# Delta-rule attention into a mixture of attention experts: the fourth unit's Gram products made during the first substitution, wide fillers and a new instruction order

## Chip, cores and metric

The kernel runs on 1 core of one Trainium2 chip. The metric is the device time in microseconds (us) of one execution. The engines are PE (matmul), DVE, ACT, POOL and SP; SP issues nearly all transfers.

## What is computed

```
k_n = k / (norm(k) + 1e-6)                          # q, k, v: [4, 8, 768, 48]
for t in range(768):
    y[t]  = q[t] @ state                            # state: 48 x 48 for each batch and head
    state = state + beta[t] * outer(k_n[t], v[t] - k_n[t] @ state)
x = y laid out as [4, 768, 384]
for e in range(4):                                  # experts with 64 features
    a   = softmax(causal(scale * (x wq[e]) (x wk[e])^T))
    out += gate[e] * (a @ (x wv[e]) @ wo[e])        # gate: softmax over the top 2 of 4 of x w_gate
```

## The kernel before

The 32 pairs of batch and head times 768 tokens are cut into **six units** n = 0 to 5. A unit is 256 tokens of half of the batch: units 0, 1, 2 are one half in order of time, units 3, 4, 5 the other half. A unit has four chunks c of 64 tokens, and its 32 tiles (8 pairs of heads times 4 chunks) lie side by side.

For each unit the kernel loads the keys (`le`) into one of three row tiles `GF[n % 3]`, so that units 0 and 3 share `GF[0]`; PE makes the Gram products of the keys of each chunk (`ga` for units 0 to 2, `gb` for 3 to 5: two calls k = 0, 1 of two chunks each); ACT brings them back into the row tile (`ge`); diagonal blocks of 32 x 32 go to a tile `DA` (`gd`, four transfers) and by a DVE transpose to `B` (`bi`); norms and the factor `aa` come from the diagonal (`nm`).

Then each 32 x 32 block is inverted by a **substitution** of 30 dependent steps. Unit 0's (`s0`) runs on DVE at the start, while nothing else can go on. Units 1 to 5 have theirs on POOL (`sv.n.0` scales, on POOL for unit 1 and on DVE for the others; `sv.n.1` to `sv.n.30` are two POOL tensor operations each, L508 and L510; `sv.1.31` masks on POOL; `sv.n.32`, in unit 2 on DVE, ends it), one unit ahead of the place where the result is wanted. Two DVE transposes (`bo` into `DG`, `tn` into `TN`) hand it to PE, and `m1`, `we`, `m2`, `me`, `tc` build the unit's inverse in the row tile.

The **scan** of a unit goes through its chunks in order, each depending on the state that the last one left: `gk` (PE: keys times queries and state), `xs` (DVE: x = v - ...), `tx` (PE), `us` (DVE, ACT), `ku` (PE), `se` (ACT: new state), `yy` (PE: outputs), `yh` and `yl` (ACT, DVE: high and low parts of the outputs into `XU[n % 2]` and `H3`), `hx` (transfers). `vs` on POOL scales v (tile `kv`) by the norms first; `lv` and `lt` load the two halves of `kv`, `lk` the keys, `lq` the queries.

The **experts** of a unit follow a unit later, woven into the next scans: `pj` (projections; `kh`, `kl` evict them as high and low parts), `pv` (values and gate; `ve`, `lg` evict), `mx` to `mo` (row maxima), `sc`, `ex`, `av` (scores, exponentials, products with v), `ft`, `fo`, `so` (output). Their weights come in by `ww` (load), `wh` (high part, ACT) and `wl` (low part, POOL L312), for seven pieces.

**Fillers**: a word `fl.k` issues k matmuls of zeros (`ZB`, bf16, 128 x 128) on PE, into a bank that nobody reads. There are 883 of them: 487 ahead of the end of the first substitution (379 in one train that spans most of it), 396 later.

**What sets the order.** The whole program is a table of 1783 words, `ORDER`, written out one word for each call of a function above; digits behind an @ are the PSUM banks. A loop at the end of `tile_kernel` runs them one by one under `manual_schedule`, so each engine and the one queue of SP execute their instructions exactly in the order of the table:

```
for word in ORDER.split():
    word, _, at_ = word.partition("@")
    name, *a = word.split(".")
    ...
    steps[name](*a)
```

An instruction that has to wait holds up everything behind it on its engine or queue. The waits themselves follow from the tiles that are read and written.

Of the kernel before, what the change touches and what calls it, by code (L numbers as in the profile page):

```python
# [899 lines left out]
```

## Time and profile before

| | us |
|---|---|
| timed runs | 426.77, 424.69, 426.94; median 426.77 |
| profiled execution | 421.56, of it 419.8 span |
| PE busy | 399.7 (95%) |
| DVE, ACT, POOL busy | 302.8, 205.7, 227.0 |

The profiled execution is 1.2% below the median of the timed runs. PE's busy time holds the fillers, so a busy PE can stand for a wait. A stage of this kernel is best seen from one `m1.n.0` (the first product with the inverse of unit n's blocks) to the next: PE meets it at 46.9, 79.0, 138.4, 187.8, 254.4 and 306.4 us for units 0 to 5, and unit 1's first scan product `gk.1.0` at 89.6.

### The profile page before, as it was taken

To read this page: it belongs to the slowest core of one execution; us is meant where nothing else is said; L and a number is where in the kernel's file an instruction comes from. 1 tells how busy PE (TensorE), PEld (TensorE's weight loads), DVE (VectorE), ACT (ScalarE), POOL (GpSimd) and SP (SyncE) were. 2 spreads that over 40 slices of the span, in tenths; PEclk is the share of its full clock that TensorE was granted. 3 is DMA by queue.
4 is the path that set the end of the run, shared out by engine and by line. 5 is a ranking of instruction groups with operands and counts; after the bars stand their busy time and mean duration, and the time that the engine had idled before them with its cause. 6 is when DMAs were issued, how large, how long until landed. Compare 5 with 4: busy or idle time off the path is not lost.

```text
span 419.8 us, 20613 instructions
## 1 busy us (share of the span) xinstructions
PE 399.7 (95%) x9119; PEld 356.3 (85%) x9119; DVE 302.8 (72%) x635; ACT 205.7 (49%) x453; POOL 227.0 (54%) x415
## 2 busy tenths in 40 slices
...
GB/s 212 244 125 132 6 61 90 199 87 174 53 153 141 140 69 58 77 142 154 213 56 43 94 21 108 103 120 4 160 173 125 52 20 13 11 16 62 4 3 75
DMA packets 81657, 39.81 MB, mean 95 GB/s; under 512 B 64992, under 2 KB 74848, under 8 KB 81568
## 3 DMA queue, kind: packets, MB, share of 16 engines
...
q8 instruction: 71, 1.16, 1.1%
...
## 4 chain that ended last, share of the span: by engine, by line
PE 73%; DVE 10%; DMA 8%; SPq 3%; issue 3%; ACT 1%; POOL 1%; DVEq 0%; ACTq 0%
PE p L199 71%; DMA bt<-in_beta_dram 2%; DVE p L460 2%; DMA qp<-in_kq_dram 2%; DVE vs L459 1%; SPq L637 1%; DVE mp L730 1%; DMA at<-in_wqk_dram 1%; PE p L814 1%; DVE qp L395 1%; DMA kv<-in_kv_dram 1%; DMA at<-in_wo_dram 1%; PE p L739 1%; DVE p L725 1%; POOL wl L312 1%
## 5 line engine op out<-in xcount | busy, mean ns | idle before, releaser
L508 POOL TENSOR_TENSOR tm<-b 128x30 f32<-128x30 f32 (+9 forms) x150 | 72.9, 486 | 28.9 <-DVE b L504 18.1
L510 POOL TENSOR_TENSOR b<-b,tm 128x30 f32<-128x30 f32 (+9 forms) x150 | 77.7, 518 | 11.8
L199 PE MATMUL p<-zb 128*128 128x128 bf16 x883 | 55.9, 222 | 4.5 <-DVE zb L316 3.3
L775 ACT ACTIVATE at<-p 128x768 f32<-128x768 f32 (+1 forms) x48 | 43.3, 917 | 31.4 <-PE p L199 14.8
L199 PEld LDWEIGHTS <-zb 128*128 128x128 bf16 x883 | 50.7, 99 | 6.5 <-DVE zb L316 3.3
L201 ACT ACTIVATE qp<-p 64x192 f32<-64x192 f32 (+1 forms) x92 | 36.9, 401 | 26.0 <-PE p L199 24.6
L730 DVE TENSOR_REDUCE mp<-p 128x2 f32<-128x1024 f32 (+3 forms) x40 | 44.4, 1115 | 2.9 <-PE p L199 1.9
L199 PE MATMUL p<-vs,at 128*64 128x65 f32 x1344 | 44.9, 223 | 0.9 <-ACT at L775 0.9
L199 PEld LDWEIGHTS p<-vs,at 128*64 128x64 f32 x1344 | 41.4, 137 | 4.4 <-issue 2.0
L395 DVE TENSOR_TENSOR qp<-p,cs 64x256 f32<-64x256 f32 x96 | 40.5, 421 | 5.8 <-PE p L199 4.1
L199 PE MATMUL p<-xu,wh 128*128 128x512 f32 (+1 forms) x168 | 40.3, 373 | 0.0
L572 POOL TENSOR_TENSOR kv<-kv,nt 128x384 f32<-128x384 f32 x24 | 19.6, 831 | 31.2 <-DMA kv<-in_kv_dram 25.7
L199 PEld LDWEIGHTS p<-xu,wh 128*128 128x128 f32 x168 | 27.8, 188 | 5.8 <-issue 0.5
L199 PE MATMUL p<-qh,kh 64*128 64x128 f32 (+1 forms) x192 | 29.1, 299 | 0.2 <-DVE mp L730 0.2
L199 PE MATMUL p<-qp 128*48 128x64 f32 (+1 forms) x768 | 26.3, 221 | 2.2 <-issue 1.9
L780 DVE TENSOR_TENSOR p<-p,km 128x512 f32<-128x512 f32 x24 | 16.6, 696 | 14.6 <-PE p L199 14.2
L199 PE MATMUL p<-qh,kl 64*128 64x128 f32 (+1 forms) x192 | 26.9, 276 | 0.0
L199 PE MATMUL p<-ql,kh 64*128 64x128 f32 (+1 forms) x192 | 26.9, 276 | 0.0
L199 PE MATMUL p<-wh,xu 128*128 128x260 f32 x144 | 26.3, 294 | 0.6 <-DVE mp L730 0.6
L199 PEld LDWEIGHTS p<-qp 128*48 128x48 f32 (+1 forms) x768 | 23.0, 123 | 4.5 <-issue 2.8
L199 PE MATMUL p<-mr,sl 64*128 64x128 f32 (+1 forms) x192 | 26.7, 274 | 0.0
L199 PE MATMUL p<-qp,kf 48*64 48x112 f32 (+1 forms) x768 | 23.8, 259 | 0.3 <-issue 0.3
...
## 6 DMA issues: line engine op xcount, KB each, us to landing
...
```

Source lines behind the costliest of these rows:

```text
L199: T.matmul(o, lhsT=a, rhs=b, start=start, stop=True, skip_group_check=True)
L201: copy = lambda o, a: S.activation(o, a, AF.Copy)
L312: G.tensor_tensor(flat(WL[w])[:, i:i + n], st(k)[:, 0:n], flat(WH[w])[:, i:i + n], op=OP.subtract)
L395: V.tensor_tensor(QP[zi(n, c) % RQ][tok(f), f, 4 * x:4 * x + 4, 0:64], gv(n, c)[r, x, :, 0:64], PMK[r, None, :].to_broadcast([64, 4, 64]), ...
L459: V.tensor_tensor(tv, t, l, op=OP.mult)
L460: V.tensor_tensor(PX[:, 0:i, i + 1:], PX[:, 0:i, i + 1:], tv, op=OP.subtract)
L508: G.tensor_tensor(tv, b[:, i:i + 1, i + 1:].to_broadcast([128, i, m]), b[:, 0:i, i:i + 1].to_broadcast([128, i, m]), op=OP.mult)
L510: G.tensor_tensor(b[:, 0:i, i + 1:], b[:, 0:i, i + 1:], tv, op=OP.subtract if n == 1 else OP.add)
L572: G.tensor_tensor(vt, vt, NRM[n % 2][:, c * NP:c * NP + NP, None].to_broadcast([128, NP, HD]), op=OP.mult)
L730: V.tensor_reduce(o[:, :, y0:y0 + per], g, axis=AXL.X, op=OP.max, negate=True)
L775: S.activation(at(n, b, y, kp)[:, :, 0:w], P8[:, b0:b0 + 2, 0:w], AF.Exp, scale=0.125)
L780: V.tensor_tensor(g, g, KM[:, None, None, :].to_broadcast([128, 2, 2, 128]), op=OP.add)
```

## The change

1. **Unit 3's Gram products.** The loads, the products and their eviction (`le.3.*`, `gb.3.*`, `ge.3.*`) move from the scans of units 0 and 1 into the first substitution. `GF[0]` holds unit 0's inverse then, so they work in a tile `HO` that shares its memory with `XU[1]`, the second unit's output tile, which is free until unit 1's first `yh`. Four transfers `gm.3.c` (128 x 512, 2048 bytes a row, 256 KB each) copy `HO` to `GF[0]` in scan 0; `XU[1]` is allocated behind the last.
2. **Wide fillers.** `ZB` becomes 512 columns wide, and `fw.k` issues k matmuls of 128 x 512. There are 227 narrow and 144 wide fillers in place of the 883: PE's matmuls fall from 5791 to 5279, its explicit weight loads from 883 to 371. The long train becomes `fw.67` and `fl.7`.
3. **A new table** of 1809 words. `gk.0.0` (unit 0's first scan product) moves from the first substitution into scan 0, behind `ku.0.0`; `ex0` (which loads ACT's exponential table) goes there too, behind `gk.0.1`. Two memsets of PSUM banks 6 and 7 become one (`zp`). The rest are moves; three are shown below.

```
-sv.1.9 sv.1.10 bo.0 sv.1.11 tn.0 tc0.2.1 fl.379@7 m1.0.0@1 sv.1.12 ...
+sv.1.10 sv.1.11 tn.0 tc0.0.0 fw.67@7 fl.7@7 m1.0.1@1 m1.0.0@4 sv.1.12 ...
 ...
-    XU = [sb(f"xu{i}", 3, 2, 2, 2, 128, dt=F32R) for i in range(2)]
+    HO = cp.tile([128, 3072], F32, name="ho", tag="xu1")
+    XU = [sb("xu0", 3, 2, 2, 2, 128, dt=F32R), None]
 ...
-    ZB = sb("zb", 128, dt=BF16)
+    ZB = sb("zb", 512, dt=BF16)
 ...
+    def hold(n, k):
+
+        if n == 3:
+            return HO[:, 1024 * k:1024 * k + 1024].rearrange("p (m s) -> p m s", m=4)
+        return GF[n % RG][:, 16 * k:16 * k + 16].rearrange("p (m t) s -> p m (t s)", m=4)
+
 ...
-    V.memset(P8[:, 7], 0.0)
+    def zp():
+        V.memset(P8[:, 6:8], 0.0)
 ...
-            mm(P8[:, BK["fl", k][0], 0:128], ZB, ZB)
+            mm(P8[:, BK["fl", k][0], 0:128], ZB[:, 0:128], ZB[:, 0:128])
+
+    def fw(k):
+        for _ in range(k):
+            mm(P8[:, BK["fw", k][0], 0:512], ZB[:, 0:128], ZB)
 ...
     def le(n, c):
+        if n > 2:
+            nc.sync.dma_start(hold(n, c // 2)[0:112, 2 * (c % 2):2 * (c % 2) + 2],
+                              kq[n, c, 0:112, 0:512].rearrange("p (a b) -> p a b", a=2))
+            return
 ...
-                    mm(P8[gr(f, p), b + x, o:o + 64], a[feat(f), p], a[feat(f), p])
+                    a = hold(n, k)[feat(f), 2 * j + x, 64 * i:64 * i + 64]
+                    mm(P8[gr(f, p), b + x, o:o + 64], a, a)
 ...
+    def gm(n, c):
+        nc.sync.dma_start(GF[0][:, NP * c:NP * c + NP].rearrange("p t s -> p (t s)"), HO[:, 512 * c:512 * c + 512])
+        if c == 3:
+            XU[1] = cp.tile([128, 3, 2, 2, 2, 128], F32R, name="xu1", tag="xu1")
+
     def ge(n, k, x):
-        copy(half(GF[n % RG], k, x), gs(n, k, x))
+        if n > 2:
+            copy(hold(n, k).rearrange("p (c x) (i j) -> p c x i j", x=2, i=4)[:, :, x], gps(n, k, x))
+            return
+        copy(half(GF[n % RG], k, x), gps(n, k, x))
```

(`gs` is renamed `gps` throughout.) In the excerpts below, line numbers behind the change are 8 to 24 higher for the same function.

**POOL, start of unit 1's substitution.** L409 (L433 behind the change) is the last work for unit 0, L572 (L596) is `vs`, L312 (L320) is `wl`, L502 (L526) is `sv.1.0`, and L508 and L510 (L532, L534) are the steps. Before:

```order
L409 TENSOR_TENSOR at1_105<-at1_105,aa0_88 128x1024 x2
L572 TENSOR_TENSOR kv0_72<-kv0_72,nt0_93 128x384
L572 TENSOR_TENSOR kv1_73<-kv1_73,nt0_93 128x384
L312 TENSOR_TENSOR wl0_133<-at2_106,wh0_130 128x512
L502 TENSOR_TENSOR b1_81<-b1_81,aa1_92 128x1024
...
L510 TENSOR_TENSOR b1_81<-b1_81,tm_84 128x4x27
L312 TENSOR_TENSOR wl0_133<-at2_106,wh0_130 128x512 x2
L572 TENSOR_TENSOR kv2_74<-kv2_74,nt0_93 128x384
```

Behind the change:

```order
L320 TENSOR_TENSOR wl0_133<-at2_106,wh0_130 128x512
L433 TENSOR_TENSOR at1_105<-at1_105,aa0_88 128x1024 x2
L596 TENSOR_TENSOR kv0_72<-kv0_72,nt0_93 128x384
L596 TENSOR_TENSOR kv2_74<-kv2_74,nt0_93 128x384
L596 TENSOR_TENSOR kv1_73<-kv1_73,nt0_93 128x384
L526 TENSOR_TENSOR b1_81<-b1_81,aa1_92 128x1024
L532 TENSOR_TENSOR tm_84<-b1_81 128x30
```

`vs.0.2` (kv2) goes from the middle of the substitution to a place ahead of it, and one `wl` ahead of L433; the other two `wl` go between later steps.

**SP's queue, the loads of the first substitution.** `gf2` and `ho` are key tiles for Gram products, `kv` values, `at2` weight pieces. Before:

```order
L350 DMA gf2_77<-in_kq_dram 112x512
L281 DMA kv0_72<-in_kv_dram 128x384
L304 DMA at2_106<-in_wqk_dram 128x512
L281 DMA kv1_73<-in_kv_dram 128x384
L277 DMA qp3_71<-in_kq_dram 64x8x64 x2
L288 DMA cs_136<-in_consts_dram 128x209
L304 DMA at2_106<-in_wqk_dram 128x512 x2
L480 DMA da_79<-gf2_77 32x32x32 x4
L281 DMA kv2_74<-in_kv_dram 128x384
```

Behind the change:

```order
L366 DMA gf2_77<-in_kq_dram 112x512
L289 DMA kv0_72<-in_kv_dram 128x384 x2
L363 DMA ho_96<-in_kq_dram 112x512
L285 DMA qp0_68<-in_kq_dram 64x8x64 x2
L363 DMA ho_96<-in_kq_dram 112x512 x2
L285 DMA qp2_70<-in_kq_dram 64x8x64 x2
L296 DMA cs_136<-in_consts_dram 128x209
L285 DMA qp3_71<-in_kq_dram 64x8x64 x2
L289 DMA kv2_74<-in_kv_dram 128x384 x2
L312 DMA at2_106<-in_wqk_dram 128x512
```

Four `ho` loads (the first of them a few rows earlier) and the kv2 pair stand ahead of the weights; `kv2` used to come behind three weight pieces and `gd`.

**DVE, from the end of unit 1's substitution to unit 2's scaling.** L467 and L470 (L491, L494) are `bo.1` and `tn.1`, L575 (L599) `xs.0.3`, L661 (L685) `kl`, L395 (L419) `pm`, L629 and L631 (L653, L655) `yl`, L426 (L450) the first of unit 2's norms, behind which `sv.2.0` comes. Before:

```order
L467 STREAM_TRANSPOSE dg_78<-b1_81 128x32x32
L470 STREAM_TRANSPOSE tn_82<-b1_81 128x32x32
L575 TENSOR_TENSOR x_95<-kv0_72,p8_63 128x384
L661 TENSOR_TENSOR kl_100<-p8_63,kh_99 128x2x128
L395 TENSOR_TENSOR qp3_71<-p8_63,cs_136 64x4x64
L661 TENSOR_TENSOR ql_102<-p8_63,qh_101 128x2x128
L395 TENSOR_TENSOR qp3_71<-p8_63,cs_136 64x4x64 x3
L595 COPY qp3_71<-p8_63 64x4x48 x2
L426 TENSOR_SCALAR g00_85<-b0_80 128x32
```

Behind the change:

```order
L491 STREAM_TRANSPOSE dg_78<-b1_81 128x32x32
L494 STREAM_TRANSPOSE tn_82<-b1_81 128x32x32
L419 TENSOR_TENSOR qp3_71<-p8_63,cs_136 64x4x64
L685 TENSOR_TENSOR kl_100<-p8_63,kh_99 128x2x128
L599 TENSOR_TENSOR x_95<-kv0_72,p8_63 128x384
L419 TENSOR_TENSOR qp3_71<-p8_63,cs_136 64x4x64 x3
L653 TENSOR_TENSOR h3_98<-p8_63,h3_98 112x2x64
L655 TENSOR_TENSOR xu0_97<-p8_63,xu0_97 112x2x3x64
L685 TENSOR_TENSOR ql_102<-p8_63,qh_101 128x2x128
L450 TENSOR_SCALAR g00_85<-b0_80 128x32
```

Two `yl` of chunk 2 come ahead of unit 2's norms, which used to stand ahead of `sv.1.32`; a further L685 stands right ahead of `sv.2.0`.

## Rows read from the trace of the kernel before

**Rows 1.** From the page: the span; the busy time, share and instructions of each engine; the shares of the chain of work that ended last.

```profile
span 419.8 us, 20613 instructions
PE 399.7 (95%) x9119; PEld 356.3 (85%) x9119; DVE 302.8 (72%) x635; ACT 205.7 (49%) x453; POOL 227.0 (54%) x415
PE 73%; DVE 10%; DMA 8%; SPq 3%; issue 3%; ACT 1%; POOL 1%; DVEq 0%; ACTq 0%
```

**Rows 2.** Busy time by stage. Columns: stretch from:to and its length in us; busy us and number of instructions of PE, PE's weight loads, DVE, ACT, POOL; granted PE clock (1.00 is full); busy share of the DMA engines; GB/s.

```profile
3.20:26.50 23.30, 21.77 (x549) 20.77 (x550) 17.49 (x43) 12.61 (x30) 12.75 (x18) 1.00 0.88 224
25.20:46.40 21.20, 21.20 (x381) 21.10 (x379) 19.09 (x51) 4.62 (x9) 18.06 (x29) 1.00 0.40 92
46.90:79.00 32.10, 30.06 (x900) 27.46 (x900) 22.21 (x35) 17.62 (x47) 27.43 (x46) 1.00 0.29 83
79.00:89.60 10.60, 10.60 (x356) 9.77 (x356) 8.96 (x27) 7.25 (x17) 5.08 (x10) 1.00 0.57 148
89.60:138.40 48.80, 46.83 (x1094) 41.43 (x1092) 40.54 (x90) 26.40 (x63) 37.99 (x70) 1.00 0.57 130
138.40:187.80 49.40, 48.44 (x1270) 42.92 (x1269) 38.73 (x77) 26.52 (x56) 37.37 (x73) 1.00 0.34 91
187.80:254.40 66.60, 64.35 (x1484) 56.55 (x1481) 55.53 (x114) 31.55 (x69) 38.26 (x72) 1.00 0.39 96
254.40:306.40 52.00, 50.77 (x1107) 44.85 (x1105) 34.27 (x70) 25.66 (x59) 38.77 (x74) 1.00 0.40 102
306.40:419.80 113.40, 106.92 (x2028) 92.73 (x2027) 64.74 (x133) 52.62 (x107) 9.69 (x20) 1.00 0.18 49
```

**Rows 3.** The timeline of DVE, ACT and POOL in the first substitution: start us, length us, engine, line, operation, output<-input, count; in brackets the idle time ahead and what ended it.

```profile
26.51 0.63 ACT L201 ACTIVATE wh<-at 128x512 fp32r<-128x512 f32 x1 [0.80 <-DMA at<-in_wqk_dram]
27.41 0.35 DVE L415 RECIPROCAL rr<-g 128x32 f32<-128x32 f32 x1 [0.39 <-ACT g L424]
29.48 2.38 POOL L502 TENSOR_TENSOR b<-b,aa 128x1024 f32<-128x1024 f32 x1 [1.49 <-DVE aa L436]
31.51 1.28 ACT L320 ACT_TABLE_LOAD   x1
```

**Rows 4.** The fillers: two trains on PE's timeline (x is how many), and, behind the dots, their group in PE's lines from 46.8 to 78.9, from 78.9 to 187.8 and from 187.8 to 419.8 us (count | busy us, mean ns of one in a pipelined engine | idle ahead).

```profile
25.14 21.33 PE L199 MATMUL p<-zb 128*128 128x128 bf16 x379
87.53 2.13 PE L199 MATMUL p<-zb 128*128 128x128 bf16 x35
...
L199 PE MATMUL p<-zb 128*128 128x128 bf16 x165 | 10.8, 220 | 0.0
L199 PE MATMUL p<-zb 128*128 128x128 bf16 x106 | 7.5, 220 | 0.0
L199 PE MATMUL p<-zb 128*128 128x128 bf16 x125 | 8.3, 220 | 0.0
```

**Rows 5.** PE's timeline where unit 3's Gram products stand before.

```profile
72.97 1.16 PE L199 MATMUL p<-gf 48*64 48x64 f32 x64 [0.96 <-DMA gf<-in_kq_dram]
91.95 1.15 PE L199 MATMUL p<-gf 48*64 48x64 f32 x63
```

**Rows 6.** The end of unit 1's substitution and its hand-over: POOL's and DVE's timeline, and, behind the dots, the pieces of the chain that ended last there (start us, us, what).

```profile
69.82 1.27 POOL L512 TENSOR_SCALAR_AFFINE_SELECT b<-b 128x1024 f32<-128x1024 f32 x1
76.34 1.92 DVE L470 STREAM_TRANSPOSE tn<-b 128x1024 f32<-128x1024 f32 x1
...
74.05 4.10 DMA at<-in_wo_dram
78.17 0.42 ACT wh L201
...
78.65 0.28 ACT vs L201
78.98 27.02 PE p L199 x770
```

**Rows 7.** The start of unit 2's substitution: DVE's, POOL's and ACT's timeline.

```profile
85.97 1.22 DVE L504 SCALAR_TENSOR_TENSOR b<-b,aa 128x1024 f32<-128x1024 f32 x1
87.51 0.29 DVE L629 TENSOR_TENSOR h<-p,h 112x128 fp32r<-112x128 f32 x1 [0.32 <-ACT xu L201]
87.72 0.55 DVE L631 TENSOR_TENSOR xu<-p,xu 112x384 fp32r<-112x384 f32 x1
88.52 0.41 DVE L661 TENSOR_TENSOR ql<-p,qh 128x256 fp32r<-128x256 f32 x1
...
85.25 1.95 POOL L565 MEMSET gf<- 32x1024 f32 x2 [5.07 <-PE p L199]
87.28 0.83 POOL L572 TENSOR_TENSOR kv<-kv,nt 128x384 f32<-128x384 f32 x1
...
87.89 0.99 ACT L201 ACTIVATE qp<-p 48x384 f32<-48x384 f32 x2
```

**Rows 8.** Two late loads: POOL's timeline ahead of unit 3's inversion, and from PE's waits (what it waited for: us in total, times, longest) the one for x.

```profile
184.87 1.62 POOL L572 TENSOR_TENSOR kv<-kv,nt 128x384 f32<-128x384 f32 x2 [4.22 <-DMA kv<-in_kv_dram]
PE p L199 <- DVE x L575: 0.8, 1, 0.8
```

**Rows 9.** PE's timeline at the start of the run.

```profile
3.27 2.74 PE L199 MATMUL p<-zb 128*128 128x128 bf16 x24 [3.27 <-DVE zb L316]
5.94 3.26 PE L199 MATMUL p<-kf 48*64 48x64 f32 x78
```

More of the change, by code (lines that the diff above doesn't have):

```diff
@@ new lines @@
+gb.4.1@45 lt.2.2 gt.0.2 lq.2.3 gt.0.3 av.0.1.1.0@1 ge.4.1.0 ra.0.0.1 gt.0.4 sv.2.32 ge.4.1.1 lk.2.0 pv.1.0.1@3
+oe.0.0.1 se.1.3.1 pj.1.2.2.0@4 nm.3.1 lg.1.0.1 ve.1.0.1 pj.1.2.2.1 gt.0.5 oe.0.1.1 se.1.3.0 pj.1.2.2.2 rb.0.0 gt.0.6
+ra.0.1.1 rb.0.1 bo.2 nr.0.0 pj.1.1.2.0@5 kh.1.2.2 pj.1.0.2.0@1 pj.1.0.2.1 vs.2.0 pj.1.0.2.2 kl.1.2.2 to.2 vs.2.2
+pj.1.3.2.0@3 tn.2 kh.1.0.2 nr.0.1 pj.1.3.2.1 ft.0.0@4 pj.1.1.2.1 vs.2.1 kl.1.0.2 pv.1.0.0@2 nm.3.2 pj.1.3.2.2 lg.1.0.0
+sv.3.0 oh.0.0 pj.1.1.2.2 ol.0.0 gk.2.0@67 sv.3.1 kh.1.1.2 sv.3.2 kh.1.3.2 m1.2.0@1 pm.2.0.0.1 ve.1.0.0 sv.3.3
@@ new lines @@
+se.3.1.0 mr.2.0.0.2 sv.4.19 se.3.1.1 mz.2.1.0.2 gk.3.2@45 ge.5.1.0 mr.2.1.0.2 ge.5.1.1 mc.2.0 xs.3.2 sv.4.20 mt.2.0@6
+gd.5 pm.3.2.1.1 mo.2.0 tx.3.2@23 pm.3.2.0.0 pm.3.2.1.0 sv.4.21 sc.2.0.0.0@67 us.3.2.1 pm.3.2.0.1 us.3.2.0
+mx.2.1.1.1@45 ex.2.0.0.0 sv.4.22 yl.3.1.0 mx.2.1.0.0@23 ku.3.2 mr.2.1.1.1 lq.3.3 yh.3.1.1 sv.4.23 mx.2.1.1.0@67
+mr.2.1.1.0 lt.4.0 sc.2.0.0.1@45 sv.4.24 lt.3.3 mr.2.1.0.0 ex.2.0.0.1 sc.2.0.0.2@67 sv.4.25 yl.3.1.1 mx.2.1.0.1@45
+sv.4.26 sm.2.0.0 mx.2.1.1.2@23 hx.3.0 av.2.0.0.0@1 mr.2.1.0.1 ex.2.0.0.2 sv.4.27 av.2.0.0.1 se.3.2.1 sv.4.28
@@ new lines @@
+mz.4.1.0.1 mr.4.1.0.1 mx.4.1.1.1@23 yh.5.2.1 yy.5.3@6 yh.5.2.0 mz.4.1.1.1 mr.4.1.1.1 av.4.0.0.0@4 yh.5.3.0 yh.5.3.1
+yl.5.2.1 sc.4.0.0.1@23 yl.5.3.1 yl.5.3.0 yl.5.2.0 sc.4.0.1.1@67 sm.4.0.0 hx.5.1 ex.4.0.0.1 mt.4.1@1 sm.4.0.1
+av.4.0.1.0@5 gt.4.3 ex.4.0.1.1 av.4.0.0.1 gt.4.2 mo.4.1 gt.4.4 av.4.0.1.1 ra.4.0.0 sc.4.1.1.0@23 oe.4.0.1 oe.4.0.0
+ra.4.0.1 rb.4.0 sc.4.1.0.0@67 gt.4.5 ex.4.1.1.0 gt.4.6 nr.4.0 sc.4.1.0.1@45 ex.4.1.0.0 pj.5.2.2.0@1 sm.4.1.0
+pj.5.2.2.1 ex.4.1.0.1 pj.5.2.2.2 pj.5.0.2.0@2 pj.5.0.2.1 pj.5.0.2.2 av.4.1.0.0@3 kh.5.0.2 kh.5.2.2 kl.5.0.2
@@ new lines @@
+ve.5.1.0 mx.5.1.0.2@23 oo.4.1.1 mx.5.1.1.0@45 mc.5.0 mz.5.1.0.2 mt.5.0@6 fo.4.1.0@1 mo.5.0 mr.5.1.0.2 gt.5.0
+sc.5.0.0.0@23 oo.4.1.0 mr.5.1.1.0 gt.5.1 so.4.1.0 sc.5.0.0.1@67 so.4.1.1 ex.5.0.0.0 sc.5.0.0.2@45 ex.5.0.0.1
+mx.5.1.1.2@23 sm.5.0.0 gt.5.2 av.5.0.0.0@1 mz.5.1.1.2 ex.5.0.0.2 sc.5.0.1.0@67 mr.5.1.1.2 mx.5.1.0.1@45 ex.5.0.1.0
+av.5.0.0.1 mr.5.1.0.1 mx.5.1.1.1@23 av.5.0.0.2 mr.5.1.1.1 mx.5.1.0.0@45 sc.5.0.1.1@67 mr.5.1.0.0 sc.5.0.1.2@23
+ex.5.0.1.1 mc.5.1 gt.5.3 mt.5.1@4 sm.5.0.1 gt.5.4 av.5.0.1.0@6 mo.5.1 gt.5.5 ex.5.0.1.2 av.5.0.1.1 gt.5.6 oe.5.0.0
@@ new lines @@
+ra.5.0.0 av.5.0.1.2 sc.5.1.0.0@23 ra.5.0.1 rb.5.0 oe.5.0.1 nr.5.0 sc.5.1.0.2@45 ex.5.1.0.0 sc.5.1.0.1@67 sm.5.1.0
+ex.5.1.0.2 ft.5.0@1 av.5.1.0.0@2 ex.5.1.0.1 sc.5.1.1.0@45 oh.5.0 ol.5.0 av.5.1.0.1 ex.5.1.1.0 av.5.1.0.2 sc.5.1.1.1@45
+ra.5.1.0 sc.5.1.1.2@67 ex.5.1.1.1 av.5.1.1.0@1 sm.5.1.1 ex.5.1.1.2 av.5.1.1.1 oe.5.1.0 av.5.1.1.2 fo.5.0.1@2 ra.5.1.1
+rb.5.1 oe.5.1.1 nr.5.1 fo.5.0.0@1 oo.5.0.1 so.5.0.1 ft.5.1@2 oo.5.0.0 oh.5.1 so.5.0.0 ol.5.1 fw.5@3 fl.7@3 fo.5.1.1@1
+fo.5.1.0@2 oo.5.1.1 so.5.1.1 oo.5.1.0 so.5.1.0
@@ L326, in zz @@
         if k < 2:
-            if k == 0:
-                V.memset(P8[:, 6], 0.0)
             for i in (k, k + 2):
@@ L400, in ae @@
         r = slice(32 * q, 32 * q + 32) if q else slice(0, 128)
-        o, a = half(AD, k, x)[r], gs(0, k, x)[r, :, :, 32 * (q % 2):32 * (q % 2) + 32]
+        o, a = half(AD, k, x)[r], gps(0, k, x)[r, :, :, 32 * (q % 2):32 * (q % 2) + 32]
         if x:
@@ L411, in al @@
     def al(k, x):
-        copy(AL[2 * k + x].rearrange("p (c i) j -> p c i j", c=2), gs(0, k, x)[:, :, :, 0:32])
+        copy(AL[2 * k + x].rearrange("p (c i) j -> p c i j", c=2), gps(0, k, x)[:, :, :, 0:32])
     def root(g0, r, ss):
```

265 lines of the change are left out of this document (120 added, 145 removed).

## The prediction

> **What bounds the kernel now.** I read the page first: PE is busy for 399.7 us of a span of 419.8, and the chain that ended last is 73% PE [rows 1]. A reader is to see a kernel bound by PE, and then to distrust it, since fillers count as busy. So I cut the span at the places where PE first uses a unit's inverse (m1.n.0) and took PE's idle time in each stage as its length less its busy time [rows 2]. From 46.9 to 79.0 us it is 32.10 - 30.06 = 2.0 us; from 79.0 to 89.6 none; then 2.0, 1.0, 2.25, 1.2 and, from 306.4 to the end, 6.5 us. Third, the fillers' rows: 396 of them behind 46.9 us. One costs 21.33 / 379 = 56.3 ns [rows 4] (the 220 ns of the lines is one in a full pipeline, not its price), so they are 22.3 us, more than PE's whole idle time of 15 us. They are what the change can give back, where they are longer than the wait that they cover. Fourth, the timelines at the hand-overs, to see which wait ends last there.
>
> So three kinds of stage: the first substitution is DVE's (busy 19.09 of 21.20 us, PE filled by one train); from 46.9 to 79.0 the clock is unit 1's substitution on POOL (27.43 of 32.10 us, with all its DVE tail behind it); from 79.0 on PE's work and the scan's chain take turns.
>
> **The change, part by part.** The sum is made against the profiled execution of 421.56 us (span 419.8); the median of the timed runs, 426.77, is 5.2 us above it, and I carry the difference over unchanged.
>
> *First substitution (to m1.0.0, 46.9 us).* Added on PE: two gb of 1.16 and 1.15 us [rows 5] and, in front of ga.2.1.0, 27 wide and 20 narrow fillers where 108 narrow stood. A wide filler isn't in the trace; it is bounded by four narrow ones, 225 ns, an estimate from the 56.3 ns above, and by one narrow one, 56 ns. I take the upper end, since its columns are four times as many. The sum, 2.3 + 7.2 - 6.1 = 3.4 us less gk.0.0's 0.7 (64 products like gb's, at most 1.16), delays the train, not DVE: the old train spans 21.33 us that DVE needs anyway. Cost 0; if that cover is gone (PE late at ga.2.1.0, whose eviction feeds unit 2), +0.5. Gained: DVE waited 0.39 us for ACT's norm, which stood behind a weight copy that waited 0.80 us for its load [rows 3]. The new order takes nm.1.0 out from behind that copy: 0 to -0.4, I take -0.4. It doesn't go into the sum, as m1.0.0 isn't what the next stage waits for.
>
> *Unit 1's substitution (to m1.1.0, 79.0 us).* POOL starts it at 29.48, after 1.49 us of waiting for DVE's aa [rows 3], and ends it at 69.82 + 1.27 = 71.09 [rows 6]. One vs (0.83 us, [rows 7]) leaves its middle for a place ahead of it, where POOL had those 1.49 us free: -0.83 at best. Against it: the moved vs waits for its load, and four ho loads stand ahead of that in SP's queue. At the 224 GB/s of the first 23 us [rows 2] the 6.2 MB queued up to it land near 31 us, at 256 GB/s near 27: 0 to +1.5 on POOL's start. Ends -1.3 and +0.4 for the end of the substitution; I take -0.3, near the middle. gb.3.0 leaves this stage: 1.16 us of work and 0.96 of waiting [rows 5], worth nothing by itself, because PE is ahead of POOL here. For the same reason gk.0.0 and ACT's table load (1.28 us, [rows 3]) cost nothing as they enter it: POOL covers them; without it they would cost 0.7 and 1.3.
>
> At the hand-over tn.1 ends at 76.34 + 1.92 = 78.26, but m1.1.0 starts at 78.98 [rows 6]. The chain shows why: a load of wo, 4.10 us to 78.15, then the ACT copy behind it, then the eviction of pv.0.0.1 whose bank m1.1.0 needs. In the new table that pv has bank 6 and the copy comes behind we.1.0, so 0 to -0.7 goes; I take -0.7, as both parts of the wait are taken apart. Late next is tn.1 itself. m1.1.0: **-1.0** (-2.0 to +0.4).
>
> *To gk.1.0 (89.6 us).* A train of 35 fillers runs until 89.66 [rows 4], though the state that gk.1.0 waits for is done at 87.89 + 0.99 = 88.88 [rows 7]. The new train is fw.4 and fl.4, 1.1 us for 2.13: **-0.7** (0 to -1.0). Added on DVE ahead of sv.2.0 are two yl and a ql, 0.29 + 0.55 + 0.41 = 1.25 us [rows 7]. Queued behind sv.2.0 is all of unit 2's substitution on POOL; but there the first step stood behind a memset that ended at 87.20 and a vs until 88.11, 0.9 us after sv.2.0 was done. vs.1.2 now comes before, so the step starts between -0.8 (the vs's time) and +0.4 (1.25 us behind 87.19, against 88.11): I take -0.5 with m1.1.0's gain in it, and nothing for the sum. The four gm transfers (256 KB each) are issued by SP in this stage and the one before, where DMA is busy at 0.29 and 0.57 [rows 2]. The last has to be done before unit 1's first yh; unit 3's row tile is needed only at its gd. 0, or +0.5 if yh waits.
>
> *To m1.3.0 (187.8 us).* gb.3.1 goes, 1.15 us [rows 5]. Fillers: the 67 left of 106 behind 89.6 us, 3.8 us, become 7 wide and 45 narrow, 4.1 us: +0.3. PE is busy for 95.3 of 98.2 us, so its work is the bound for the most part: **-0.8** (0 to -1.2). The one late load, POOL idle for 4.22 us on kv at 184.87 [rows 8], is issued earlier and its vs moves up.
>
> *To the end.* 125 fillers [rows 4], 7.0 us, become 12 wide and 47 narrow, 5.4 us: **-1.7** (0 to -2.5; the low end with the 0.8 us wait for x [rows 8], behind a late kv load). The other work of PE is the same in number.
>
> Sum: -1.0 - 0.7 - 0.8 - 1.7 = **-4.2 us**: 417.4 for a profiled execution, **422.5** as a median. A change under 0.5%, 2.1 us, can't be told from none.
>
> **Rivals.** *The waits were real (same).* Fillers fill waits. If the substitutions on POOL, 37.99 of 48.80 and 37.37 of 49.40 us [rows 2], set the hand-overs, shorter trains only turn into idle PE, and only -1 us at m1.1.0 stays: 425.8. For it: PE never idles much at a hand-over because a train sits there. Against: the one train that I could hold against its wait, before gk.1.0, was 0.8 us too long.
>
> *PE slows down (slower).* The long train shrinks from 21.33 us to at most 67 x 225 + 7 x 56 ns = 15.5 us. It starts 2.7 us later than 25.14, so it ends near 43.4, and m1.0.0 waits until about 46.5: PE idle for some 3 us. The only such idle time in these rows is at the start: behind 3.27 us, 24 fillers took 2.74 us, 114 ns each where the long train's took 56.3, and 78 products 3.26 us, 42 ns each against 18 for gb's [rows 5, 9]. Against 24 x 56.3 ns and 78 x 18 ns that is 3.2 us lost at most; I take 2.4 for a fall, as some of the 78 wait for loads. For it: 114 is twice 56, as between 1.2 and 2.4 GHz. Against: the granted clock there reads 1.00 [rows 2]. One fall ahead of m1.0.0 and two in the thinner later trains cost 7.2 - 4.2 = +3: about 430. It decides from the second fall on, where the gain is used up. The Trainium skill, "TensorE: Matmul & The Clock Gate", "Why this matters for your kernels", speaks for this rival: it tells one to leave no longer PE idle gaps between bursts, as the clock then drops to half. By the rows alone, which show 1.00 in all stages, the sum stays -4.2; by that rule it becomes +3. No row here shows a fall in the middle of a run.
>
> *More goes (faster).* If the two kv waits and half of the last stage's 6.5 us of idle time go as well, -7: 419.8.
>
> *It doesn't take hold.* If the Gram loads land late in the first substitution, PE stalls at gb.3 with ga.2.1.0 and unit 2 behind it; the train then just shrinks, and this ends like the first rival.
>
> **How the numbers follow.** Forecast 0.52, first rival 0.22, slowdown 0.14, more 0.12. Faster by over 0.5% holds the forecast except a tail of 0.03 and the third rival: 0.61. Same holds the first rival and that tail: 0.25. Slower: 0.14. The range must leave out at most 0.2. Its low end, 418, takes in the third rival and the low bounds of the substitution and the last stage; its high end, 428.5, takes in the first rival with the +0.4 and +0.5 of late loads and yh, and one fall of 2.4; two falls or more lie outside.
>
> **What would show it.** In the changed profile: m1.1.0 about 1.0 us earlier, with tn.1 as the last wait and not an eviction; sv.1's end near 70.8; a wide filler near 225 ns in a train; gk.1.0 1.7 us earlier and released by the state's eviction; no gb.3 behind 46.9 us; m1.3.0 2.5 us earlier; PE's busy time lower by some 3 us in the last three stages together at no more idle time. Wrong would be: a POOL start past 30.5 us on kv, idle PE grown by as much as the trains shrank, or fillers and products of twice their length behind the long train's end.

## The result: 0.4 to 0.8% slower, with PE at half clock in three places

| | before | after |
|---|---|---|
| median of 20 timed runs, us | 424.86 (421.2 to 430.3) | 427.06 (424.5 to 428.7) |
| ratio, 95% interval | | **1.0079** [1.0059, 1.0099] |
| profiled execution, its span, us | 421.56, 419.8 | 426.00, 424.3 |
| mean granted clock of PE, profiled | 1.00 | 0.983 |
| mean granted clock, timed runs | 0.992 (141 runs, made beside the experiments) | 0.983 (20 runs) |

The ratio compares the fast runs of either kernel; over all 20 runs the medians are 0.5% apart and the means, 425.01 and 426.73, 0.4%. The forecast was 422.5, the range to 428.5: the median lies inside the range, but the time moved the other way than forecast. The page of the changed kernel: its span, engines, granted clock in 40 slices, and chain.

```profile
span 424.3 us, 19608 instructions
PE 403.0 (95%) x8607; PEld 337.6 (80%) x8607; DVE 301.7 (71%) x634; ACT 207.1 (49%) x453; POOL 226.4 (53%) x415
PEclk9999799999999999998999999999998999999999
PE 77%; DVE 10%; issue 3%; DMA 3%; SPq 3%; ACT 3%; POOL 1%; DVEq 0%; ACTq 0%; POOLq 0%
```

PE is busy for 3.3 us *more* than before [rows 1], although it got fillers worth several us less. The 7 and the two 8s in the clock row say why. The stages (columns as in [rows 2]; cut at the same events):

```profile
28.70:46.90 18.20, 16.06 (x119) 7.92 (x110) 16.79 (x42) 3.54 (x7) 15.70 (x28) 1.00 0.37 82
46.90:80.00 33.10, 33.07 (x801) 26.10 (x801) 20.46 (x34) 17.26 (x43) 26.72 (x45) 0.90 0.35 100
80.00:90.00 10.00, 9.75 (x324) 8.30 (x323) 9.43 (x29) 8.33 (x20) 4.58 (x5) 1.00 0.39 114
90.00:140.90 50.90, 49.08 (x1063) 42.26 (x1060) 41.62 (x92) 26.98 (x64) 40.05 (x80) 1.00 0.51 122
140.90:188.40 47.50, 46.85 (x1230) 40.99 (x1222) 35.88 (x74) 25.48 (x53) 36.16 (x68) 1.00 0.40 100
188.40:258.00 69.60, 66.26 (x1441) 55.85 (x1435) 55.64 (x113) 31.82 (x69) 38.77 (x73) 0.98 0.47 111
258.00:309.10 51.10, 50.14 (x1095) 43.88 (x1091) 34.84 (x73) 27.56 (x63) 38.66 (x74) 1.00 0.30 80
309.10:424.30 115.20, 108.61 (x2017) 93.58 (x2013) 65.26 (x132) 51.78 (x104) 9.72 (x20) 0.98 0.19 50
```

Unit 1's substitution, the stage from m1.0.0 to m1.1.0, has a mean clock of 0.90 and PE busy without a gap, where before PE idled for 2.0 us. Read closer, the three stretches and, behind the first two, what follows:

```profile
47.80:54.50 6.70, 6.70 (x104) 4.29 (x98) 1.38 (x3) 3.28 (x9) 6.15 (x10) 0.50 0.01 4
54.60:61.30 6.70, 6.70 (x207) 5.41 (x207) 3.90 (x10) 4.03 (x10) 5.92 (x11) 1.00 0.35 105
191.20:194.50 3.30, 3.25 (x29) 3.02 (x31) 3.21 (x5) 0.77 (x2) 1.47 (x2) 0.50 0.91 215
194.60:197.90 3.30, 3.30 (x155) 3.07 (x152) 2.95 (x12) 2.63 (x7) 0.05 (x1) 1.00 0.71 132
317.50:320.70 3.20, 3.20 (x41) 2.97 (x39) 0.76 (x2) 1.63 (x4) 1.62 (x2) 0.50 0.53 89
```

In the first, third and fifth row the granted clock is 0.50, the lower of the two levels, 1.2 GHz. Together these falls last 13.6 us (6.8, 3.4 and 3.4), so at most half of that, 6.8 us of PE's time, is lost. PE's timeline shows what it did ahead of each (start us, length us, what; in brackets the idle time ahead and what ended it):

```profile
29.73 15.03 PE L200 MATMUL p<-zb 128*128 128x512 bf16 x74
46.93 1.39 PE L200 MATMUL p<-gf,os 32*32 32x32 f32 x64 [2.17 <-DVE gf L491]
...
189.46 0.21 PE L200 MATMUL p<-tn,gf 32*32 32x32 f32 x1 [0.78 <-DVE tn L494]
...
316.77 0.99 PE L200 MATMUL p<-qp 128*48 128x64 f32 x23 [3.18 <-issue]
```

It idled: 2.17 us between the end of the wide train (44.76) and m1.0, 0.78 and soon another 0.47 at unit 3's hand-over, 3.18 us at 313.6. The Trainium skill ("TensorE: Matmul & The Clock Gate", "Why this matters for your kernels") warns that idle gaps between bursts drop the clock to half; here the trace agrees in kind, with 2.17 us of idle time ahead of 6.8 us at 0.50, and differs in size: this gap, and the 0.78 and 0.47 us at the hand-over, are shorter than those that the page warns of.

### The profile page after: what moved, and what is told of

Its sections match the earlier page's. It is cut to its first block, busy times and chain, and to the rows that moved or that the text cites. A ratio compares the mean times of both kernels' runs of the same rounds, so it can differ in the third digit from the quotient of the medians.

```text
span 424.3 us, 19608 instructions
## 1 busy us (share of the span) xinstructions
PE 403.0 (95%) x8607; PEld 337.6 (80%) x8607; DVE 301.7 (71%) x634; ACT 207.1 (49%) x453; POOL 226.4 (53%) x415
## 4 chain that ended last, share of the span: by engine, by line
PE 77%; DVE 10%; issue 3%; DMA 3%; SPq 3%; ACT 3%; POOL 1%; DVEq 0%; ACTq 0%; POOLq 0%
PE p L200 75%; DVE p L484 2%; SPq L661 2%; DVE vs L483 2%; PE p L838 1%; DVE mp L754 1%; DMA out_dram<-ot 1%; DMA kv<-in_kv_dram 1%; PE p L763 1%; DVE qp L419 1%; ACT qp L202 1%; DVE p L749 1%; ACT at L799 1%; DMA qp<-in_kq_dram 1%; SPq L289 1%
## 5 line engine op out<-in xcount | busy, mean ns | idle before, releaser
L532 POOL TENSOR_TENSOR tm<-b 128x30 f32<-128x30 f32 (+9 forms) x150 | 72.8, 485 | 27.9 <-DVE b L528 17.3
L534 POOL TENSOR_TENSOR b<-b,tm 128x30 f32<-128x30 f32 (+9 forms) x150 | 77.6, 517 | 11.8
L200 PE MATMUL p<-zb 128*128 128x128 bf16 (+1 forms) x371 | 52.9, 296 | 5.3 <-DVE zb L324 2.9
L200 PEld LDWEIGHTS <-zb 128*128 128x128 bf16 x371 | 29.0, 104 | 26.5 <-issue 6.0
L419 DVE TENSOR_TENSOR qp<-p,cs 64x256 f32<-64x256 f32 x96 | 40.3, 420 | 10.5 <-PE p L200 5.6
L200 PE MATMUL p<-vs,at 128*64 128x65 f32 x1344 | 46.0, 223 | 0.7 <-ACT at L799 0.7
L596 POOL TENSOR_TENSOR kv<-kv,nt 128x384 f32<-128x384 f32 x24 | 19.7, 832 | 33.9 <-DMA kv<-in_kv_dram 32.9
L200 PE MATMUL p<-wh,xu 128*128 128x260 f32 x144 | 27.4, 302 | 0.5 <-DVE qp L619 0.5
L619 DVE COPY qp<-p 64x192 f32<-64x192 f32 x48 | 17.0, 354 | 14.1 <-PE p L200 13.1
```

The costliest lines, as they stand in the source:

```text
L200: T.matmul(o, lhsT=a, rhs=b, start=start, stop=True, skip_group_check=True)
L419: V.tensor_tensor(QP[zi(n, c) % RQ][tok(f), f, 4 * x:4 * x + 4, 0:64], gv(n, c)[r, x, :, 0:64], PMK[r, None, :].to_broadcast([64, 4, 64]), ...
L532: G.tensor_tensor(tv, b[:, i:i + 1, i + 1:].to_broadcast([128, i, m]), b[:, 0:i, i:i + 1].to_broadcast([128, i, m]), op=OP.mult)
L534: G.tensor_tensor(b[:, 0:i, i + 1:], b[:, 0:i, i + 1:], tv, op=OP.subtract if n == 1 else OP.add)
L596: G.tensor_tensor(vt, vt, NRM[n % 2][:, c * NP:c * NP + NP, None].to_broadcast([128, NP, HD]), op=OP.mult)
L619: V.tensor_copy(o, a)
```

## The experiments

Line numbers are not needed: an edit is a word of the table, shown as a difference. Beside each ratio to runs of the kernel before made in the same session (95% interval) stand the span and the mean clock of its one profiled execution.

**1. Fillers put back where PE idled ahead of each fall, one place at a time.** e1_train:

```
-fw.67@7 fl.7@7
+fw.77@7 fl.7@7
```

> The long train in front of m1.0.0 gets 10 more wide fillers (2.15 us), so that PE's 2.17 us of idle time there goes; nothing else is changed. Clock theory: no stretch at half clock behind 47 us (6.8 us long in the changed kernel), the stage from m1.0 to gk.0.1 shrinks from 10.8 to about 8 us, m1.1.0 comes 1 us earlier (what follows is bound by POOL and DVE, tn.1 ended at 78.95), and the time falls by about 1 us (0.5 to 3.4). Order theory (the new order's own waits set the time, the clock is hidden): m1.1.0 and the time within 0.5 us of the changed kernel's.

**1.0056** [1.0024, 1.0088]; 421.5, 0.996. No fall at 47 us and none at 317; one remains, at 197.4 (3.4 us). gk.0.1 comes 7.85 us behind m1.0.0 in place of 10.81, as expected. Of these 3.0 us, 1.1 are left at m1.1.0: all but two of its products wait for tn.1, until 78.97. By the ratios e1 is 1.0 us faster than the changed kernel, which is what was expected, but the intervals overlap. e2_unit3:

```
-yl.2.2.0 m1.3.0@1 ... pv.2.0.1@2
+yl.2.2.0 fw.4@1 m1.3.0@1 ... fw.2@3 pv.2.0.1@2
```

> Six wide fillers at unit 3's hand-over: four in front of m1.3.0, two in front of pv.2.0.1, where PE idled 0.78 and 0.47 us. Clock theory: no stretch at half clock at 191 us (3.4 us long), gk.3.1 comes 1.7 us earlier against m1.3.0, and the time falls by 1 to 1.7 us. Order theory: the stage is set by waits for DVE and ACT, the time is the same within 0.5 us.

**1.0046** [1.0012, 1.0080]; 423.2, 0.984. No fall at 191 us; those at 46 (10.2 us) and 315 (3.4) stay. gk.3.1 comes 0.7 us earlier against m1.3.0, less than the 1.7 expected. e3_unit5:

```
-lv.5.1 m1.5.1@1
+lv.5.1 fw.12@1 m1.5.1@1
```

> Twelve wide fillers in front of m1.5.1, ahead of the 3.18 us in which PE waited for nothing that the trace shows and which I read as waiting for its next piece of code. Clock theory: no stretch at half clock at 317 us, PE's idle time there down to 1 us or less, gk.5.0 no later (about 321) and the work behind it faster, the time 1 to 1.7 us lower. If the wait isn't a late load of code, the fillers push yy.4.3 back by their 2.6 us and the time rises by up to 2.6 us.

**1.0036** [0.9994, 1.0077]; 423.2, 0.992. No fall at 317 us; 47 and 81 (3.4 us each) show one. So each place that got cover is without a fall in its run. But uncovered places change as well: e1 has no fall at 317, e3 none at 191 and a new one at 81. One execution of each therefore proves little about the two later places.

Ahead of m1.0.0 all 18 profiled executions of this case can be laid side by side. With 0.94 us of idle time or less there (12 of them) no fall follows; 1.24 us (e8 below) and 1.50 us (e3) are followed by 3.4 us at half clock, 1.59 us (e7) by none, 2.17 us (the changed kernel) by 6.8, 2.26 us (e2) by 10.2, 3.59 us (e5) by 13.6. And in the new order gk.0.1 comes 7.85 us behind m1.0.0 where no fall stands (e1, e4, f1 to f4), 9.29 and 9.34 us where one of 3.4 us does (e3, e8), 10.81 with 6.8 us of it and 12.25 with 10.2. So the fall of 6.8 us costs **3.0 us** up to that place. e4_all makes the three edits together:

> The fillers of the three runs before together. Clock theory: granted clock 0.99 or more, and the time lower by the sum of the three, 3 to 5 us, so that it is at or a little below the kernel before (ratio 0.995 to 1.000). Order theory: as the changed kernel, ratio 1.006 to 1.010.

**1.0040** [1.0002, 1.0078]; 419.9, 1.000. In its profiled execution no stretch before the end is at half clock, and it is 424.3 - 419.9 = 4.4 us shorter than the changed kernel's. That compares one execution of each. Over its timed runs e4 has a mean clock of 0.990, so falls come back, and the mean is only 1.2 us (+-0.7) below the changed kernel's (425.58 against 426.73); the ratio lies between the two expectations. The rows of the profiled execution:

```profile
PE 402.9 (96%) x8635; PEld 335.7 (80%) x8635; DVE 302.6 (72%) x634; ACT 207.0 (49%) x453; POOL 226.7 (54%) x415
PEclk9999999999999999999999999999999999999999
```

419.9 is also before's 419.8: even with the falls gone, none of the -4.2 is there. The 28 wide fillers that bought this are 18 x 0.218 = 3.9 us behind m1.0 (the other 10 lie beside DVE). So in that execution the clock was held for nearly the fillers that had been counted as given back. In e8_more three further places get some:

```
-m2.3.0@45 ... gb.4.0@67 ... m1.1.0@4
+fw.9@4 m2.3.0@45 ... fw.5@6 gb.4.0@67 ... fw.4@4 m1.1.0@4
```

> The kernel of the run with all three groups of fillers, with three more: 9 wide ones in front of m2.3.0 (ahead of a 2.0 us wait that I read as a late piece of code), 5 in front of gb.4.0, 4 in front of m1.1.0. Clock theory: mean clock at or above 0.994 (0.990 without them), and the time 1 to 1.7 us lower than there, ratio to before 0.998 to 1.002. If the wait isn't for code, the nine fillers add up to 1.9 us.

1.0023 [0.9994, 1.0052], just above the ratio expected; 423.8, 0.996, with a fall at 49 us (3.4 us). Over its timed runs the mean clock is 0.997, the highest of all, but PE is busy for 407.3 us where e4 has 402.9:

```profile
PE 407.3 (96%) x8632; PEld 339.0 (80%) x8653; DVE 303.2 (72%) x634; ACT 207.2 (49%) x453; POOL 227.2 (54%) x415
```

More cover keeps the clock up and costs about as much as it keeps.

**2. Does before's own order fall too?** e5_b_cut only shortens its long train:

```
-fl.379@7
+fl.340@7
```

> The kernel before with 39 fillers less in the long train (340 for 379, 2.2 us), so that PE idles some 2.6 us ahead of m1.0.0, as in the changed kernel; nothing else is changed. Clock theory: a stretch at half clock begins near 47 us, the mean granted clock falls by about 0.008 (6.8 us at half), and the time rises by 1 us (unit 1's substitution on POOL hides the rest) to 3.4 us. Order theory: the idle time costs nothing, the time is within 0.5 us of before.

**1.0107** [1.0071, 1.0143]; 428.2, 0.976. PE idles for 3.59 us ahead of m1.0, then:

```profile
46.83 1.38 PE L199 MATMUL p<-gf,os 32*32 32x32 f32 x44 [3.59 <-DVE gf L467]
...
46.10:59.70 13.60, 12.87 (x275) 11.91 (x276) 5.10 (x9) 6.64 (x17) 12.11 (x20) 0.50 0.07 17
```

13.6 us at 0.50 (two falls of 3.4 us follow at 114 and 323). gk.0.1 comes 4.9 us later than before and m1.1.0 3.6 us, although POOL, not PE, had set that stage: its cover hides only a part. The 1.07% are 4.5 us, more than the 1 to 3.4 expected. So before's own order falls as soon as its train is shorter; the new order isn't needed for it. e9_b_cover, the other way, covers before's idle places (`fl.379` to `fl.389`, `fl.18` to `fl.33`, `fw.4`, `fw.8` and `fw.9` at three hand-overs):

> The kernel before with more fillers where PE idled in its trace and nothing else: 10 and 15 narrow ones at the ends of the trains ahead of m1.0.0 and m1.1.0, 4 wide ones ahead of gb.3.0 (it waits 0.96 us for its load), 8 ahead of m2.1.1 and 9 ahead of m2.5.0 (each within the piece of code whose end shows a wait of 1.72 and 1.92 us). The kernel before has a mean granted clock of 0.992 over its timed runs, and its time falls by 3.1 us for each 0.01 of clock among those runs. Clock theory: clock 0.996 or more, time 1 to 2.4 us lower than before (ratio 0.994 to 0.998). If PE's work is the bound where I put them, they add up to 2 us.

**1.0099** [1.0066, 1.0133]; 429.1, 0.988: a miss. PE now waits 4.30 us in the middle of a scan for "issue", where before's longest such wait is 1.92 us, and the clock falls there. This asked for experiments 5.

```profile
201.26 0.68 PE L199 MATMUL p<-wh,xu 128*128 128x260 f32 x2 [4.30 <-issue]
...
200.00:206.70 6.70, 5.43 (x23) 5.34 (x23) 2.58 (x8) 0.90 (x4) 3.09 (x10) 0.50 0.23 48
```

**3. Are wide fillers at fault?** e7_b_wide replaces before's trains by wide ones of the same length:

```
-fl.379@7
+fw.<as many as take the same time>@7 fl.<rest>@7      (each train alike)
```

> The kernel before in its own order, with part 2 of the change alone: every train of fillers made of wide ones (215 ns each) up to its old length, the rest narrow. If wide fillers are as good as narrow ones for the clock, time and mean clock are those of before (within 0.5 us and 0.002). Rival: the wide ones are at fault for the clock, and it falls below 0.990 with 1 to 3 us more. With some 1,300 PE instructions less there are about 10 pieces of code less to load, and the waits that I read as code waits (1.72 and 1.92 us) stand elsewhere.

0.9980 [0.9951, 1.0008]; 420.5, 0.996; over the timed runs a mean clock of 0.993, where before has 0.992. They are not: within this interval wide fillers hold the clock as well as narrow ones of the same length.

**4. The hoist alone.** e6_b_gb is before's order with unit 3's loads, products and evictions in the first substitution and the four transfers behind:

```
-fl.379@7
+fl.190@7 gb.3.0@23 ge.3.0.1 ge.3.0.0 fl.40@7 gb.3.1@23 ge.3.1.0 ge.3.1.1 fl.108@7 wh.3
```

> The kernel before in its own order and with its narrow fillers, with part 1 of the change alone: unit 3's Gram products in the first substitution (inside the long train, which gives up 41 fillers for them), held in the second unit's row tile, copied back by four transfers in scan 0. My sum says -1.15 us for gb.3.1 and nothing for gb.3.0, if no wait is new: 0.4 to 1.2 us faster. Rival: the loads and the four transfers crowd SP's queue, a load behind them comes late: 0.5 to 2 us slower.

**1.0091** [1.0044, 1.0138]; 424.2, 0.996: about twice the loss that the rival allowed. Where gb.3.0 stood, PE now waits for POOL (waits of PE: total, times, longest):

```profile
PE p L199 <- POOL wl L319: 2.7, 2, 1.4
PE p L199 <- issue: 9.3, 9, 2.1
```

gb.3.0 was worth nothing there, as forecast. The second row was not foretold: from m1.3.0 to gk.3.1 PE idles for 3.6 us, in two waits for "issue" of 1.45 and 2.15 us. e11_b_gb_align keeps the edit and only takes 87 products out of a train of the same length:

```
-fl.190@7
+fl.72@7 fw.31@7
```

> The run with the hoist alone, with 118 narrow fillers of the long train replaced by 31 wide ones (both 6.7 us): 87 PE products less, so that the products behind the train stand at the same places in PE's 128-product pieces of code as in the kernel before (there they were 41 places off). Nothing else is changed. Code theory: the waits of 1.45 and 2.15 us at unit 3's hand-over, which stand at the 4,548th and 4,676th product, go, gk.3.1 comes 2.5 to 3 us earlier against m1.3.0, and the time is 2 to 3 us lower than of the hoist alone. Rival (the hoist's transfers or the clock cause those waits): the waits stay at the same words, the time within 1 us of the hoist alone.

1.0031 [1.0001, 1.0060]; 423.1, 0.988. That stage is 17.5 us, not 21.1, its idle time 0.3 us. e11's mean is 2.3 us (+-1.0) below e6's, so most of e6's loss went with the number of products; the hoist is left at +0.3%, and gains nothing.

**5. The number of products.** PE's waits for "issue" end at fixed numbers of products from the start, whatever work stands there. Two of them, in the order before, in e5 (39 products less), e6 (other work) and e12: the products up to the wait, then the wait.

```profile
0.00:107.00 107.00, 99.11 (x2640) 92.89 (x2641) 81.02 (x182) 54.08 (x127) 80.32 (x135) 1.00 0.52 132
108.01 1.09 PE L199 MATMUL p<-gf 48*64 48x64 f32 x59 [1.72 <-issue]
...
0.00:312.50 312.50, 297.57 (x7348) 267.84 (x7349) 242.26 (x513) 157.24 (x357) 218.18 (x396) 1.00 0.45 113
313.32 0.44 PE L199 MATMUL p<-qp 128*48 128x64 f32 x9 [1.92 <-issue]
```

```profile
0.00:113.50 113.50, 103.38 (x2640) 96.64 (x2641) 82.03 (x184) 54.29 (x127) 82.79 (x138) 0.94 0.50 124
0.00:321.00 321.00, 303.28 (x7348) 273.21 (x7349) 242.06 (x515) 158.38 (x359) 218.97 (x396) 0.97 0.45 111
```

```profile
0.00:191.00 191.00, 179.76 (x4548) 163.32 (x4549) 150.14 (x327) 97.55 (x224) 140.32 (x249) 0.99 0.50 125
191.59 1.11 PE L199 MATMUL p<-zb 128*128 128x128 bf16 x17 [1.45 <-issue]
...
0.00:318.50 318.50, 299.39 (x7347) 268.62 (x7348) 242.17 (x514) 157.80 (x359) 218.18 (x396) 0.99 0.47 116
```

```profile
0.00:110.00 110.00, 99.65 (x2639) 91.71 (x2641) 82.99 (x184) 53.81 (x127) 82.97 (x138) 1.00 0.51 128
0.00:319.50 319.50, 301.09 (x7347) 269.53 (x7349) 243.19 (x515) 157.51 (x359) 218.53 (x396) 0.99 0.45 112
```

2640 and 7348 within one, at times up to 7 and 9 us apart. (The row of e6 above is of a third such wait, behind 4548; its wait behind 2639 is there too, 1.18 us up to 109.28.) The queue that carries the instructions moved 71 packets before, 67 after: 9119 / 71 = 128.4 and 8607 / 67 = 128.5 products for each.

```profile
q8 instruction: 71, 1.16, 1.1%
```

```profile
q8 instruction: 67, 1.10, 1.2%
```

So the waits look like waits for pieces of the program, some 128 products each. The packets settle it as far as a trace can: the 18 traces have 68 waits of PE for "issue" of over 0.5 us, and every one ends 1.17 to 1.64 us behind the end of a packet of this queue (16,384 bytes each), while the packets of before come 5.7 us apart on average. No run took the loading itself away. That the count matters is shown by runs that change it, with the length of the train kept. e12_b_m32 and e13_b_m96 put wide fillers for narrow ones in before's long train, at the same length:

```
-fl.379@7
+fl.336@7 fw.11@7        (e12: 32 products less)
+fl.249@7 fw.34@7        (e13: 96 less)
```

> The kernel before with 43 narrow fillers of the long train replaced by 11 wide ones (both 2.4 us): 32 PE products less ahead of everything behind the train, nothing else (the memset of the filler tile is 0.2 us longer). Code theory: waits that end at a border of PE's code stay at the same number of the product (2,640 and 7,348 in the kernel before, give or take 3) and so fall on other work, 32 products later; their sizes change, and the time moves by up to 1% either way with them and with the clock. Rival (the order alone sets the waits): they stay at the same words, gb.4.0 and yy.4.3, and the time is within 0.3% of before.

> The same with 130 narrow fillers replaced by 34 wide ones (both 7.3 us): 96 products less, 32 more than a whole piece of 128 would leave. Code theory: as the run with 32 less, the waits at the same numbers of the product and at other words than there, the time different from it by up to 1%. Rival: both runs and before within 0.3% of each other.

1.0033 [1.0003, 1.0063] and **1.0079** [1.0051, 1.0108]; spans 426.7 and 426.0. Against e7's 0.998, which has wide fillers in that train too, the fillers' width isn't the cause. Waits for "issue" add up to 10.1 and 9.2 us, against 6.0 before; e13's longest is 3.35 us. So before loses by a shift of its borders in both runs. The change is another matter: its 512 products less are close to four whole pieces (71 packets less 67), and the two borders named first fall into the same words as before, gb.4.0 (behind 2257 products, a wait of 0.83 us) and yy.4.3 (behind 6836, 3.18 us).

The rival that this left: the new order *has* its gain and only lies badly on the borders. Four kernels lay e4's order elsewhere, by 25, 48, 76 and 99 products, covering most of one spacing:

```
-fw.77@7 fl.7@7
+fw.68@7 fl.41@7         (f1; f2: fw.60 fl.72; f3: fw.50 fl.110; f4: fw.42 fl.141)
```

> The changed kernel with the three groups of fillers, and 9 wide ones of the long train replaced by 34 narrow ones (both 1.9 us): everything behind the train stands 25 PE products later. Code theory: the waits stay at the numbers 2,257 and 4,292 (give or take 3) and fall on other words; the time moves by up to 1% against the run without the shift. If the new order holds the forecast gain, one of the four shifts is at a ratio of 0.990 to 0.997; if it holds none, all lie at 1.000 to 1.010.

> The same with 17 wide fillers replaced by 65 narrow ones: 48 products later. Expected as for the shift by 25.

> The same with 27 wide fillers replaced by 103 narrow ones: 76 products later. Expected as for the shift by 25.

> The same with 35 wide fillers replaced by 134 narrow ones: 99 products later. Expected as for the shift by 25.

1.0073 [1.0041, 1.0106], 1.0060 [1.0023, 1.0097], 1.0051 [1.0019, 1.0083], 1.0039 [1.0007, 1.0071]. All lie where the expectation put a new order without the gain, none is clearly below e4's 1.0040, and the mean clock is 0.990 to 0.992 in all. That rival falls, as far as five places tell.

## Why the prediction was wrong, step by step

**The failed step is the idle time ahead of m1.0.0, foretold at some 3 us and put into the sum at nothing:** "By the rows alone, which show 1.00 in all stages, the sum stays -4.2", in the rival "PE slows down". The wait came, 2.17 us, and PE's clock fell behind it, for 6.8 us that cost 3.0 us up to gk.0.1; e5 shows that the shorter train alone does it. The rows were of one execution at clock 1.00, and the timed runs of before were not like it: their mean clock is 0.992, and over the timed runs of all kernels here that have a clock on record (343, each kernel with its own level) a run takes 3.13 +- 0.15 us more for each 0.01 of clock. The only sign of this ahead of the forecast were the 5.2 us between profile and median, "carried over unchanged"; 0.008 of clock accounts for some 2.4 of them. And the one argument against the rival was a misreading: "the granted clock there reads 1.00" is of a stretch, 3.20 to 26.50 us, whose clock is on record only from 8.5 us on, and what isn't on record counts as 1.00 in that column. The fillers from 3.27 us on started 107 ns apart, those behind 10.4 us 56 ns apart. Fillers that look 0.8 us too long against their wait were also what kept the clock.

The difference of the means, 426.73 - 424.46 = 2.27 us (before's over the 141 runs; 1.7 against the 20 of the result, whose clock isn't on record), can be split with that slope, as an estimate: the clock went from 0.9922 to 0.9826, 0.96 steps of 3.13 us: **+3.0 us**; at equal clock **-0.7** (+-0.3) is left. Within the changed kernel's own 20 runs the slope is only 1.7 +- 0.6, so the +3.0 may be too large and the -0.7 a loss. The rival had a chance of 0.14, and its +3 was +2.3. Its count, one fall ahead of m1.0 and two later, came true partly by luck: it put the later two down to thinner trains, but the one at 317 us stands behind 3.18 us in which PE waited for its program, and the runs with fillers show them at other places. Its price, 2.4 us, was 3.0 for the first. So two things were off: the falls (0 put in, +3.0) and the gain (-4.2 put in, -0.7).

| point reached, us | before | after | e4 | foretold | got |
|---|---|---|---|---|---|
| unit 1's first scaling, POOL | 29.48 | 30.97 | 29.43 | 0 to +1.5 | +1.49 |
| end of unit 1's substitution | 71.09 | 71.56 | 70.03 | -0.3 | +0.47 |
| m1.1.0 | 78.98 | 80.03 | 76.22 | -1.0 | +1.05 |
| gk.1.0 | 89.59 | 90.07 | 88.40 | -1.7 | +0.48 |
| m1.3.0 | 187.83 | 188.44 | 187.26 | -2.5 | +0.61 |
| end | 419.8 | 424.3 | 419.9 | -4.2 | +4.5 |

m1.1.0 and m1.3.0 are taken at their first product. In the new order two of their products can go ahead of the others; m1.3.0 of the changed kernel goes on at 189.46.

*First substitution: partly right.* A wide filler costs (15.03 - 7 x 0.0563) / 67 = 218 ns (taken: 225), the two gb took 2.10 us (taken: 2.3). The train ended at 44.76 (foretold 43.4) and PE idled 2.17 us (foretold some 3). That this idle time costs nothing was wrong.

*Unit 1's substitution: partly right.* POOL's start has moved to its upper bound, since the moved vs waited for its load; the end (+0.47) and m1.1.0 (+1.05) lie past theirs of +0.4.

```profile
29.40 1.62 POOL L596 TENSOR_TENSOR kv<-kv,nt 128x384 f32<-128x384 f32 x2 [1.29 <-DMA kv<-in_kv_dram]
30.97 2.36 POOL L526 TENSOR_TENSOR b<-b,aa 128x1024 f32<-128x1024 f32 x1
...
70.29 1.27 POOL L536 TENSOR_SCALAR_AFFINE_SELECT b<-b 128x1024 f32<-128x1024 f32 x1
```

So a profiled start past 30.5 us, one of the signs named for a miss, is there; it was not what decided, for e4 has the start at 29.43 and ends level with before. The eviction ahead of m1.1.0 is gone, as foretold: PE waits there for nothing, since it is busy to the end. But it is busy because the fall had put it behind: gk.0.1 comes 10.81 us behind m1.0.0, and 7.85 us where no fall stood (e1, e4). In e4 m1.1.0 starts 2.76 us earlier than before; two of its products go then, and the others wait until 77.27 for tn.1, the last wait that was foretold, which is 1.7 us earlier. The step was right in sign and in kind, and 1.0 was too small.

*gk.1.0: the fillers' term was right.* The train's end and gk.1.0 in the changed kernel:

```profile
88.88 1.26 PE L200 MATMUL p<-zb 128*128 128x512 bf16 x8
90.07 0.61 PE L200 MATMUL p<-qp,kf 48*64 48x112 f32 x16
```

1.26 us of fillers stand for 2.13 [rows 4]: -0.87 (taken: -0.7), and gk.1.0 starts 0.06 us behind the state's eviction, which ends at 90.01. But unit 2's first step on POOL, foretold 0.5 us earlier, starts at 90.20 against 88.07, 2.1 us later: vs.1.2 is out of its way, as foretold, but the memset ahead of it (85.25 before [rows 7]) now starts at 88.18, after 3.24 us of waiting for PE.

*To m1.3.0 and to the end: wrong.* -0.8 and -1.7 were counted as PE's work less fillers. PE's busy time in the last three stages rose from 222.0 [rows 2] to 66.26 + 50.14 + 108.61 = 225.0 us, where some 3 us less was foretold; the two falls there, 6.8 us at half clock, account for at most 3.4 of it. Without falls, e4 gains 0.57 us at m1.3.0 and none at the end, with 3.9 us of fillers more; but against the changed kernel at equal clock, by the slope above, these fillers cost 1.3 us (422.57 against 421.29, +-0.4), so the rest of them covers waits. So the first rival, that fillers fill waits, is borne out for much of the giveback; how much, the runs do not tell. The third (more goes) did not come: of the two kv waits the one of 4.22 us [rows 8] is gone, and the end did not move for it.

What stays open: how the 3.5 us that are missing at equal clock divide between waits that took the fillers' place and a poorer place among the borders of the program's pieces (single waits of up to 3.2 us here, 1.9 before, but 6.5 and 6.0 us in all), and why 0.78 and 0.47 us of idle time went ahead of a fall at 191 us while 1.92 us at 313 before did not.
